# Delta-rule attention with two expert layers on one core: a shorter VectorE narrowing of the second part's weights, and later transposes

## The chip, the cores and the metric

The kernel runs on one core of a Trainium2 chip. The time is the device time of one execution in microseconds (us), and the number compared is the median of a few runs. The profile shows a single execution, so its span differs a little from the median. TensorE does the matrix products, VectorE (DVE) and ScalarE (ACT) the element-wise work on tiles in SBUF and PSUM, GpSimd (POOL) element-wise work in SBUF and some DMA issues, SyncE (SP) issues the other DMAs.

## The reference

The reference has three stages, cut here to what is computed. Inputs are `q`, `k`, `v` of 4 x 8 x 768 x 48, the weights `w_in` (384 x 2048), `w_out` (2048 x 384), `w_gate` (384 x 8), and `w1`, `w2` of eight experts. The dense weights come out of the reference's set-up as 64-bit floats; the other inputs are 32-bit.

```
for t in range(768):                       # 32 pairs of batch and head
    y[t]  = q[t] @ state
    state = state + beta[t] * outer(k_n[t], v[t] - k_n[t] @ state)
x = y as 3072 tokens x 384
h = x @ w_in
g = h * clip(h + 3, 0, 6) / 6
x = g @ w_out
logits = x @ w_gate                        # one expert per token: argmax
out[token] = gate * (relu(x @ w1[e]) @ w2[e])
```

## The kernel before, in words

Products that must be exact to 32 bits are made from a high and a low half: each weight and each activation is split into `H` (rounded by a ScalarE copy to the type that TensorE takes in one pass) and `L` (the rest, by a subtraction on GpSimd or VectorE), and three products H·H, H·L and L·H are added in PSUM.

The dense layer has 16 blocks of 128 of its 2048 hidden columns. The first seven (`NF1`) are multiplied in the first part of the program, beside the recurrence, for all tokens; their sum goes to the memory tensor `ypart`. The second part (from line 1298) does the other nine (`NF2` = 9) for six blocks of 512 tokens each. These six are called block 0 to block 5 below, the nine are rounds f = 0 to 8. A round makes `ph`, nine gate products of 512 columns on TensorE (lines 1316 to 1321), then `t` on ScalarE and VectorE, `gH` on ScalarE and `gL` on VectorE (1323 to 1328), and, two rounds later (`SK` = 2), twelve output products into the four `py` banks (1329 to 1336). After the last round `gather` adds `ypart` (1229) and `route` sorts the 512 tokens into the experts' slots. Then come the eight experts.

The weights arrive as 64-bit floats. `narrow` (lines 172 to 185) turns one tile of 128 x 384 of them into 32-bit floats: a DMA on SP's queue brings both halves into a `stage` tile (a ring of four), ScalarE writes the absolute value of the high words into an `nw` tile (a ring of three), and four VectorE operations follow: a maximum that bounds the exponent from below, a shift left by three with a mask, an operation that puts the top bits of the high word back, and one that adds the top three bits of the low word. `weights` (187 to 208) does one block: it narrows the `w_in` tile and splits it into `wiH` and `wiL` (ScalarE, GpSimd); narrows the `w_out` tile and splits it into `woH` and `woL`; transposes it on TensorE (`pwt`, three transposes) and copies the result to `wt` on ScalarE; and multiplies it with the router's weights (`pwc`, six products), copies eight columns (`wc`, VectorE) and splits those into the last columns of `woH` and `woL`. So each block is four steps, ended by the word "part". In the multiplication of the first seven blocks `narrow_first` does the same narrowing in another way: a scaled absolute value on ScalarE, a multiplication of the high words by zero on GpSimd, and two VectorE operations.

Of the nine blocks of the second part the first three (`NP` = 3) are prepared at the tail of the first part by `ahead_stream`, with `tags[0]` = "st". The other six (f = 3 to 8) are prepared in block 0's loop by `prepare` (tags[0] = "rst"): in round f, ahead of the gate products, block f+3 takes its first step, block f+2 its second, block f+1 its third and block f its fourth. Both use the same rings.

Each engine works through its instructions in a fixed order, which is made when the program is built. In the first part the order of the named streams is written out by hand (`ORDER`). Elsewhere a planner goes by the order of the text, and lets an instruction go ahead of an earlier one that it expects not to be ready; so instructions of `prepare` can stand between those at the tail of the first part. The expert weights (`load_expert`) are loaded into the same ring of stage tiles after the last narrowing.

Of the kernel before, what the change touches and what calls it, by code (L numbers as in the profile page):

```python
# [7 lines left out]
FP32 = mybir.dt.float32  # L8
# [4 lines left out]
ACTF = mybir.ActivationFunctionType  # L13
ALU = mybir.AluOpType
# [57 lines left out]
def kernel(ctx: ExitStack, tc: tile.TileContext, q, k, v, beta, w_in, w_out, w_gate, w1, w2, out):  # L72
# [21 lines left out]
    PE, ACT, DVE, POOL, DMA = [Defer(n, e) for n, e in (("pe", pe), ("act", act), ("dve", dve), ("pool", pool), ("dma", nc.sync))]  # L94
# [75 lines left out]
    def narrow(src_ap, sp, tags):  # L170

        t_ = sp.tile([128, 384, 2], I32, tag=tags[0], name="stage", bufs=tags[1])
        src = src_ap.bitcast(I32)
        if len(src.shape) == 3:
            yield DMA.dma_start(out=t_.rearrange("p (c f) two -> p c (f two)", c=src.shape[1]), in_=src)
        else:
            yield DMA.dma_start(out=t_.rearrange("p f two -> p (f two)"), in_=src)
        b_ = sp.tile([128, tags[4]], I32, tag=tags[2], name="nw", bufs=tags[3])[:, 0:384]
        bf = b_.bitcast(FP32)
        yield ACT.activation(bf, t_.bitcast(FP32)[:, :, 1], ACTF.Abs)  # L180
        yield DVE.tensor_scalar(bf, bf, 2.0 ** -15, None, ALU.max)
        yield DVE.tensor_scalar(b_, b_, 3, 0x3FFFFFFF, ALU.logical_shift_left, ALU.bitwise_and)
        yield DVE.scalar_tensor_tensor(b_, t_[:, :, 1], -(1 << 30), b_, ALU.bitwise_and, ALU.bitwise_or)
        yield DVE.scalar_tensor_tensor(b_, t_[:, :, 0], 29, b_, ALU.logical_shift_right, ALU.bitwise_or)
        return bf

    def weights(f, di, do, sp, tags, take, give):

        fs = slice(f * 128, (f + 1) * 128)
        t_ = yield from narrow(w_in.bitcast(I32).rearrange("(c p) f -> p c f", p=128)[:, :, f * 256:(f + 1) * 256], sp, tags)  # L190
        yield from split_ops(di, t_.rearrange("p (c f) -> p c f", c=KD))
        yield "part"
        t_ = yield from narrow(w_out[fs, :], sp, tags)
        yield from split_ops([x[:, 0:DM] for x in do], t_)
        yield "part"
        p_ = yield from take("pwt", t_)
        yield [PE.transpose(p_[:, c * 128:(c + 1) * 128], t_[:, c * 128:(c + 1) * 128], ident) for c in range(KD)]
        wt = sp.tile([128, tags[7]], FP32, tag=tags[5], name="wt", bufs=tags[6])[:, 0:DM]
        yield ACT.activation(wt, p_[:, 0:DM], ACTF.Copy)
        give(p_)  # L200
        yield "part"
        p2 = yield from take("pwc", wt)
        yield [PE.matmul(p2[:, 0:E], wt[:, c * 128:(c + 1) * 128], wg[:, c], start=c == 0, stop=c == KD - 1) for c in range(KD)]
        wc = sp.tile([128, E], FP32, tag="wc", name="wc")
        yield DVE.tensor_copy(wc, p2[:, 0:E])
        give(p2)
        yield from split_ops([x[:, DM:YW] for x in do], wc)
# [3 lines left out]
    NP = 3  # L211
# [809 lines left out]
    def bank(name):  # L1021
        return ps.tile([128, 512], FP32, tag="ps", name=name)
# [55 lines left out]
    def load_xt(rw, xt):  # L1078
        n = sum(height(rw))
        for c in range(KD):  # L1080
            p_ = bank("pxe")[:, 0:n]
            for t, r_ in enumerate(rw):
                m = r_.shape[0]
                pe.transpose(p_[:, t * 128:t * 128 + m], r_[:, c * 128:(c + 1) * 128], ident[0:m, 0:m])
            act.activation(xt[0][:, c, 0:n], p_, ACTF.Copy)
            dve.tensor_tensor(xt[1][:, c, 0:n], p_, xt[0][:, c, 0:n].bitcast(FP32), ALU.subtract)
        return xt
# [50 lines left out]
    def step(gen, n):  # L1138
        for _ in range(n):
            r = next(gen, None)  # L1140
            if r is not None:
                ready[id(gen)] = r
        return ready.get(id(gen))

    pre = load_expert(0, "a")
    with mx:
# [36 lines left out]
        def wi(x, f):  # L1183
            return (ahead["wi"][x][:, :, f * 128:(f + 1) * 128] if f < NP else wi1[x][:, :, (f - NP) * 128:(f - NP + 1) * 128])

        def wo(x, f):
            return ahead["wo"][x][:, f] if f < NP else wo1[x][:, f - NP]
# [4 lines left out]
        def load_x(b):  # L1192
            xt = x_tiles(b)
            for x in range(2):
                pool.dma_start(out=xt[x], in_=xd[x].rearrange("(c p) t -> p c t", p=128)[:, :, b * 512:(b + 1) * 512])
            return xt
# [9 lines left out]
        def prepare(f, parts=1):  # L1206

            if f not in range(NP, NF2):
                return
            if f not in prep:  # L1210
                prep[f] = weights(NF1 + f, [wi(x, f) for x in range(2)], [wo(x, f) for x in range(2)], wr,
                                  ("rst", 4, "rnw", 3, 384, "rwt", 2, DM), bank_now, lambda p_: None)
            for op in prep[f]:
                if op == "part":
                    parts -= 1
                    if not parts:
                        return
                    continue
                for o in (op if isinstance(op, list) else [op]):
                    o.now()  # L1220
# [66 lines left out]
        def pad_first():  # L1287

            pk = bank("pad")
            pe.matmul(pk[:, 0:E], oneb, cnt, start=True, stop=True)  # L1290
            pad = rp.tile([1, E], FP32, tag="pad", name="pad", bufs=1)
            dve.tensor_scalar(pad, pk[0:1, 0:E], -1.0, float(FIRST), ALU.mult, ALU.add)
            padb = const.tile([128, E], BF16, name="padb")
            dve.memset(padb, 0.0)
            dve.tensor_scalar(padb[0:1, 0:1], pad[:, 0:1], 0.0, None, ALU.max)
            counts.append(padb)

        row, first = None, {}
        for b in range(NT // 512):
            xt = nxt  # L1300
            if b + 1 < NT // 512:
                nxt = load_x(b + 1)
            if b == 1:
                step(pre, 1)
            py = [bank(f"py{t}") for t in range(4)]
            pend = []
            for f in range(NF2 + SK):
                if f == SK + 1 and row is not None:
                    step(route(b - 1, row), 2)
                if b > 1 and f % 2:  # L1310
                    step(pre, 1)
                if b == 0:
                    for n in range(4):
                        prepare(f + NP - n)
                if f < NF2:
                    ph = bank("ph")
                    n = 0
                    for c in range(KD):
                        for a, x in ((0, 0), (0, 1), (1, 0)):
                            pe.matmul(ph, wi(a, f)[:, c], xt[x][:, c], start=n == 0, stop=n == 3 * KD - 1)  # L1320
                            n += 1
                    t_ = gp.tile([128, 512], FP32, tag="t", name="t")
                    act.activation(t_, ph, ACTF.Relu, bias=half, scale=1.0 / 6.0)  # L1323
                    dve.scalar_tensor_tensor(t_, t_, 1.0, ph, ALU.min, ALU.mult)  # L1324
                    gH = gp.tile([128, 512], FP32R, tag="gH", name="gH", bufs=SK + 1)
                    gL = gp.tile([128, 512], FP32R, tag="gL", name="gL", bufs=SK + 1)
                    act.activation(gH, t_, ACTF.Copy)  # L1327
                    dve.tensor_tensor(gL, t_, gH.bitcast(FP32), ALU.subtract)  # L1328
                if f >= SK:
                    fp, gh, gl = pend.pop(0)  # L1330
                    for t in range(4):
                        ts_ = slice(t * 128, (t + 1) * 128)
                        o = py[t][:, 0:YW]
                        pe.matmul(o, gh[:, ts_], wo(0, fp), start=fp == 0, stop=False)  # L1334
                        pe.matmul(o, gh[:, ts_], wo(1, fp), start=False, stop=False)  # L1335
                        pe.matmul(o, gl[:, ts_], wo(0, fp), start=False, stop=fp == NF2 - 1)  # L1336
                if f < NF2:
                    pend.append((f, gH, gL))
                if b == NT // 512 - 1:
                    if f == SK + 1:  # L1340
                        pad_first()
                    if f == SK + 4:
                        first["rows"] = load_rows(0, slots, 0, FIRST, rp, "row2")
                    if f == NF2 - 1:
                        first["xt"] = load_xt(first["rows"], x_tiles(b + 1))
            row = gather(b, py)
# [144 lines left out]
```

## Time and profile before

| what | us |
|---|---|
| median of three runs (960.23 to 964.41) | 963.11 |
| time of the profiled execution | 965.32 |
| span of the profiled execution, first to last instruction | 963.6 |
| TensorE busy | 871.2 |
| VectorE busy | 575.1 |
| ScalarE busy | 549.3 |
| GpSimd busy | 440.8 |

Busy times are sums over instructions; products overlap, and a busy TensorE is not one at its peak. The chain that ended last is followed back from the last instruction, at each step to what released it. The granted clock is a share of 2.4 GHz: 1.00 is 2.4, 0.50 is 1.2. Nearly all operations of the helpers carry line 36, so they are told apart by tile names.

### The profile page before, as it was taken

What the parts mean: (1) busy time and instruction counts of PE and PEld (TensorE: products, weight loads), DVE (VectorE), ACT (ScalarE), POOL (GpSimd) and SP (SyncE); (2) the same over time, 40 slices, a digit from 0 to 9 for tenths busy, and PEclk for the clock granted to TensorE, in tenths of its full rate; (3) what the DMA queues carried; (4) which work ended last, traced back from release to release, by engine and by line L of the source; (5) the groups of instructions that cost most, each with busy time, mean ns of one, the idle gap of its engine ahead of it and who ended that gap; (6) DMA issues with size and microseconds to landing.
All of it is one profiled execution on the core that took longest, in us unless ns stands there. A gap on an engine that the chain in (4) does not pass through costs nothing.

```text
span 963.6 us, 27622 instructions
## 1 busy us (share of the span) xinstructions
PE 871.2 (90%) x11570; PEld 812.9 (84%) x11570; DVE 575.1 (60%) x1493; ACT 549.3 (57%) x1105; POOL 440.8 (46%) x423
## 2 busy tenths in 40 slices
PE   2425889999989999989899999999999999999996
PEld 2324889989989999988778988989899999999996
DVE  7898999979879797654785365554452221122221
ACT  5858888788978867655565333332325454255521
POOL 6676656455635424323441140321116744775751
PEclk9999999999999999999999999999999999999999
DMA  8789999999888767873653342241318633544400
GB/s 151 150 161 153 162 186 153 169 185 158 168 151 175 173 153 167 180 237 101 198 184 108 106 149 66 101 127 40 118 60 273 219 92 117 176 125 126 161 21 21
DMA packets 250918, 137.83 MB, mean 143 GB/s; under 512 B 195427, under 2 KB 235685, under 8 KB 250784
## 3 DMA queue, kind: packets, MB, share of 16 engines
q1 hardware_dynamic: 242960, 117.77, 53.7%
q0 software_dynamic: 7280, 17.41, 5.6%
q8 instruction: 92, 1.51, 0.7%
q10 hardware_dynamic: 544, 0.80, 0.2%
q14 instruction: 42, 0.34, 0.1%
HBM read 71.56 MB, written 35.50 MB: 111 GB/s over the span
## 4 chain that ended last, share of the span: by engine, by line
PE 73%; DVE 9%; issue 6%; ACT 5%; POOL 4%; DMA 1%; SPq 1%; POOLq 0%; ACTq 0%
PE ph L1320 11%; PE ph L1111 9%; PE ph L36 8%; PE py L36 8%; PE py L1335 4%; PE py L1334 4%; PE py L1336 4%; PE pz L1099 3%; PE pz L1101 3%; PE pz L1100 3%; PE pO L36 3%; PE pW L36 3%; DVE nw L36 2%; PE pP L36 2%; DVE nws L36 1%
## 5 line engine op out<-in xcount | busy, mean ns | idle before, releaser
L1115 DVE SCALAR_TENSOR_TENSOR hL<-ph,hH 128x384 fp32r<-128x384 f32 (+6 forms) x64 | 36.1, 564 | 163.5 <-ACT hH L1114 161.4
L36 POOL TENSOR_TENSOR gL<-t,gH 128x512 fp32r<-128x512 f32 (+1 forms) x48 | 56.3, 1174 | 108.8 <-ACT gH L36 80.7
L1114 ACT ACTIVATE hH<-ph 128x384 fp32r<-128x384 f32 (+6 forms) x64 | 31.6, 494 | 105.2 <-PE ph L1111 105.2
L1280 POOL DMA_INDIRECT slots<-row,di x24 | 23.9, 996 | 125.1 <-DVE di L1272 119.6
L1323 ACT ACTIVATE t<-ph,half 128x512 f32<-128x512 f32 x54 | 37.1, 688 | 75.8 <-PE ph L1320 71.2
L36 PE MATMUL ph<-xTH,wiH 128*128 128x256 f32 x252 | 75.3, 299 | 1.1 <-DVE t L36 1.0
L1324 DVE SCALAR_TENSOR_TENSOR t<-t,ph 128x512 f32<-128x512 f32 x54 | 37.1, 686 | 64.3 <-ACT t L1323 55.5
L1132 POOL DMA_INDIRECT out_dram<-yo,rw x29 | 28.1, 968 | 100.7 <-ACT yo L1131 96.4
L1099 PE MATMUL pz<-a2H,hH 128*128 128x384 f32 (+1 forms) x216 | 73.2, 339 | 0.4 <-ACT hH L1114 0.4
L1100 PE MATMUL pz<-a2L,hH 128*128 128x384 f32 (+1 forms) x216 | 72.4, 335 | 0.0
L1101 PE MATMUL pz<-a2H,hL 128*128 128x384 f32 (+1 forms) x216 | 72.4, 335 | 0.0
L36 PE MATMUL ph<-xTL,wiH 128*128 128x256 f32 x252 | 71.9, 285 | 0.2 <-DVE xTL L36 0.2
L36 PE MATMUL ph<-xTH,wiL 128*128 128x256 f32 x252 | 71.7, 285 | 0.0
L1328 DVE TENSOR_TENSOR gL<-t,gH 128x512 fp32r<-128x512 f32 x54 | 46.6, 864 | 32.7 <-ACT gH L1327 32.5
L36 DVE TENSOR_TENSOR Xp<-Xp,sub 128x31 f32<-128x31 f32 (+15 forms) x186 | 64.0, 344 | 2.7
L36 DVE TENSOR_TENSOR sub<-Bt,Xp 128x31 f32<-128x31 f32 (+15 forms) x186 | 62.0, 333 | 3.2
L152 POOL TENSOR_TENSOR a2L<-r,a2H 128x384 fp32r<-128x384 f32 x64 | 62.5, 1008 | 0.0
L36 PE MATMUL py<-woH,gH 128*128 128x392 f32 x168 | 61.0, 363 | 0.0
L152 POOL TENSOR_TENSOR a1L<-r,a1H 128x512 fp32r<-128x512 f32 x48 | 60.4, 1301 | 0.1
L36 PE MATMUL py<-woL,gH 128*128 128x392 f32 x168 | 57.6, 343 | 1.8 <-issue 1.8
L1111 PE MATMUL ph<-yTL,a1H 128*128 128x384 f32 (+5 forms) x168 | 58.3, 347 | 0.0
L1111 PE MATMUL ph<-yTH,a1L 128*128 128x384 f32 (+5 forms) x168 | 58.3, 347 | 0.0
(323 smaller groups left out, 3066.3 us busy)
## 6 DMA issues: line engine op xcount, KB each, us to landing
r<-in_moe_w_dram SPq DMA_DIRECT2D x32, 768.0 KB, 4.5
slots<-zrow SPq DMA_DIRECT2D x8, 784.0 KB, 5.5
stage<-in_moe_w_out_dram SPq DMA_DIRECT2D x16, 384.0 KB, 4.7
stage<-in_moe_w_in_dram SPq DMA_DIRECT2D x16, 384.0 KB, 3.6
row<-ypart SPq DMA_DIRECT2D x6, 784.0 KB, 4.4
ysave<-row SPq DMA_DIRECT2D x6, 784.0 KB
rw<-slots SPq DMA_DIRECT2D x24, 196.0 KB, 3.0
kr<-in_k_dram SPq DMA_DIRECT2D x24, 192.0 KB, 4.6
```

Of the source, the lines that this page charges most:

```text
L36: return self.fn(*self.a, **self.k)
L152: in_order(pool.tensor_tensor(dst[1], src_ap, dst[0].bitcast(FP32), ALU.subtract))
L1099: pe.matmul(o, hh[:, ts_], a2[0][:, fp], start=fp == 0, stop=False)
L1100: pe.matmul(o, hh[:, ts_], a2[1][:, fp], start=False, stop=False)
L1101: pe.matmul(o, hl[:, ts_], a2[0][:, fp], start=False, stop=fp == KF2 - 1)
L1111: pe.matmul(ph, a1[a][:, c, fs], xt[x][:, c, 0:n], start=k == 0, stop=k == 3 * KD - 1)
L1320: pe.matmul(ph, wi(a, f)[:, c], xt[x][:, c], start=n == 0, stop=n == 3 * KD - 1)
L1323: act.activation(t_, ph, ACTF.Relu, bias=half, scale=1.0 / 6.0)
L1328: dve.tensor_tensor(gL, t_, gH.bitcast(FP32), ALU.subtract)
L1334: pe.matmul(o, gh[:, ts_], wo(0, fp), start=fp == 0, stop=False)
L1335: pe.matmul(o, gh[:, ts_], wo(1, fp), start=False, stop=False)
L1336: pe.matmul(o, gl[:, ts_], wo(0, fp), start=False, stop=fp == NF2 - 1)
```

## The change

For the six blocks prepared in block 0's loop the narrowing is done as in the first part: the absolute value is scaled by 2 to the -112 on ScalarE, GpSimd multiplies the high words by zero in place, which leaves their top bit, and VectorE shifts the scaled value and joins that bit in one operation, then joins the low word's bits as before. Two VectorE operations per tile go, one GpSimd operation comes. In block 0's rounds the third and fourth step (transposes and router products) are issued behind the gate products and their `t`, `gH`, `gL` instead of ahead of them.

```diff
@@ narrow
-        yield ACT.activation(bf, t_.bitcast(FP32)[:, :, 1], ACTF.Abs)
-        yield DVE.tensor_scalar(bf, bf, 2.0 ** -15, None, ALU.max)
-        yield DVE.tensor_scalar(b_, b_, 3, 0x3FFFFFFF, ALU.logical_shift_left, ALU.bitwise_and)
-        yield DVE.scalar_tensor_tensor(b_, t_[:, :, 1], -(1 << 30), b_, ALU.bitwise_and, ALU.bitwise_or)
+        hi = t_.bitcast(FP32)[:, :, 1]
+        if tags[0] == "rst":
+            yield ACT.activation(bf, hi, ACTF.Abs, scale=2.0 ** -112)
+            yield POOL.tensor_scalar(hi, hi, 0.0, None, ALU.mult)
+            yield DVE.scalar_tensor_tensor(b_, b_, 3, t_[:, :, 1], ALU.logical_shift_left, ALU.bitwise_or)
+        else:
+            yield ACT.activation(bf, hi, ACTF.Abs)
+            yield DVE.tensor_scalar(bf, bf, 2.0 ** -15, None, ALU.max)
+            yield DVE.tensor_scalar(b_, b_, 3, 0x3FFFFFFF, ALU.logical_shift_left, ALU.bitwise_and)
+            yield DVE.scalar_tensor_tensor(b_, t_[:, :, 1], -(1 << 30), b_, ALU.bitwise_and, ALU.bitwise_or)
         yield DVE.scalar_tensor_tensor(b_, t_[:, :, 0], 29, b_, ALU.logical_shift_right, ALU.bitwise_or)
@@ the loop over the rounds
                 if b == 0:
-                    for n in range(4):
+                    for n in range(2):
                         prepare(f + NP - n)
                 if f < NF2:
                     ph = bank("ph")
...
                     dve.tensor_tensor(gL, t_, gH.bitcast(FP32), ALU.subtract)
+                if b == 0:
+                    for n in range(2, 4):
+                        prepare(f + NP - n)
                 if f >= SK:
```

## Rows read from the trace of the kernel before

**Rows 1.** The page: busy time by engine, and the chain's shares by engine.
```profile
PE 871.2 (90%) x11570; PEld 812.9 (84%) x11570; DVE 575.1 (60%) x1493; ACT 549.3 (57%) x1105; POOL 440.8 (46%) x423
PE 73%; DVE 9%; issue 6%; ACT 5%; POOL 4%; DMA 1%; SPq 1%; POOLq 0%; ACTq 0%
```
**Rows 2.** The chain in order of time (start us, us, what): starts of blocks 0, 1, 2.
```profile
469.65 4.47 PE ph L1320 x18
...
518.49 6.30 PE ph L1320 x27
...
557.11 6.30 PE ph L1320 x27
```
**Rows 3.** The chain, 486 to 507: the transposes' release, and two groups of gate products.
```profile
486.68 1.25 DVE nw L36
...
487.98 0.55 PE pwt L36 x3
488.53 0.57 PE pwc L36 x6
489.10 3.52 PE ph L1320 x9
...
504.96 2.19 PE ph L1320 x9
```
**Rows 4.** Waits (us in total, times, longest): 455 to 515, 469 to 519, 518 to 963.
```profile
PE pwt L36 <- DVE nw L36: 4.6, 4, 2.4
...
PE pwt L36 <- DVE nw L36: 2.2, 3, 1.9
...
PE pz L1099 <- ACT hH L1114: 0.4, 1, 0.4
```
**Rows 5.** Stretches: length, busy PE, PEld, DVE, ACT, POOL, then granted clock.
```profile
486.00:488.00 2.00, 0.10 (x2) 0.03 (x1) 1.97 (x5) 1.51 (x5) 1.56 (x2) 1.00 0.39 117
...
490.00:493.00 3.00, 3.00 (x9) 2.41 (x8) 2.92 (x8) 0.63 (x2) 0.00 (x0) 0.50 0.24 81
```
**Rows 6.** The chain at the tail of the first part, 460 to 470.
```profile
461.23 2.57 DVE nw L36 x3
...
463.93 0.52 PE pwt L36 x3
...
466.81 0.43 ACT gH L36
...
467.30 0.74 POOL gL L36
...
469.10 0.51 ACT yp L36
```
**Rows 7.** VectorE groups, 459 to 505 (busy us, mean ns), and the stretch 479.4 to 488.
```profile
L36 DVE TENSOR_SCALAR nw<-nw 128x384 int32<-128x384 int32 x13 | 7.8, 615 | 0.1
L36 DVE TENSOR_SCALAR nw<-nw 128x384 f32<-128x384 f32 x13 | 5.4, 426 | 0.4 <-ACT nw L36 0.4
...
479.40:488.00 8.60, 6.70 (x39) 5.92 (x38) 8.50 (x18) 4.21 (x11) 3.66 (x4) 1.00 0.40 126
```
**Rows 8.** By tile `stage`, whole span: ns min/median/max, first and last start.
```profile
L36 DVE SCALAR_TENSOR_TENSOR nw<-stage,nw x36: 544/554/1618, 413.8 to 503.2; 128x384 int32<-128x384 int32 x36
L36 ACT ACTIVATE nw<-stage x18: 534/544/557, 411.1 to 497.0; 128x384 f32<-128x384 f32 x18
...
L36 ACT ACTIVATE nws<-stage x14: 523/544/554, 10.8 to 111.9; 128x384 f32<-128x384 f32 x14
L36 POOL TENSOR_SCALAR stage<-stage x14: 1192/1220/2066, 11.4 to 115.5; 128x384 f32<-128x384 f32 x14
L36 DVE SCALAR_TENSOR_TENSOR nws<-nws,stage x14: 534/555/1345, 13.1 to 120.9; 128x384 int32<-128x384 int32 x14
```
**Rows 9.** GpSimd groups, 475.4 to 506: busy us, mean ns, idle before.
```profile
L36 POOL TENSOR_TENSOR woL<-nw,woH 128x384 fp32r<-128x384 f32 x5 | 5.2, 1047 | 3.6 <-ACT woH L36 3.6
L36 POOL TENSOR_TENSOR wiL<-nw,wiH 128x384 fp32r<-128x384 f32 x4 | 4.4, 1096 | 15.6 <-ACT wiH L36 15.6
L36 POOL TENSOR_TENSOR woL<-wc,woH 128x8 fp32r<-128x8 f32 x5 | 1.7, 336 | 0.1
```
**Rows 10.** Instructions in order of time, VectorE then GpSimd, 460 to 463.
```profile
460.14 0.35 DVE L36 TENSOR_SCALAR nw<-nw 128x384 f32<-128x384 f32 x1
...
461.70 1.62 DVE L36 SCALAR_TENSOR_TENSOR nw<-stage,nw 128x384 int32<-128x384 int32 x1
...
461.43 1.47 POOL L36 TENSOR_TENSOR gL<-t,gH 128x512 fp32r<-128x512 f32 x1 [2.02 <-ACT gH L36]
```
**Rows 11.** In order of time: ScalarE, GpSimd; then pieces of the chain.
```profile
478.57 1.43 ACT L36 ACTIVATE nw<-stage 128x384 f32<-128x384 f32 x3
...
482.53 1.00 POOL L36 TENSOR_TENSOR wiL<-nw,wiH 128x384 fp32r<-128x384 f32 x1 [7.20 <-ACT wiH L36]
504.42 1.00 POOL L36 TENSOR_TENSOR woL<-nw,woH 128x384 fp32r<-128x384 f32 x1 [2.24 <-ACT woH L36]
...
493.22 0.52 ACT wiH L36
...
507.14 0.18 PE py L1334
```

## The prediction

> **What bounds the kernel now.** I read the page's busy shares and its chain of waits first. TensorE is busy for 90% of the span and carries 73% of the chain that ended last [rows 1]. So a saving counts only where TensorE stands still, and the question is where it does so because of the narrowing that the change touches. The chain in order of time gives the three starts that matter: block 0 of the second part begins at 469.65, block 1 at 518.49, block 2 at 557.11 [rows 2]. Block 0 takes 48.84 us, block 1 38.62. Block 0 has six transpose groups (0.55 us) and six groups of router products (0.57) that block 1 has not [rows 3], 6 x 1.12 = 6.72. That leaves 48.84 - 38.62 - 6.72 = 3.50 us of lost time in block 0.
>
> The waits say where it goes. TensorE stands 2.2 us in three pieces, 1.9 the longest, before the transposes `pwt`, each time for the VectorE narrowing of `nw` [rows 4]. The long piece ends at 487.98, straight behind a narrowing instruction of VectorE. After it the granted clock is 0.50 in 490 to 493 (the 1.2 GHz level), after a stretch of 2 us in which TensorE was busy for 0.10 us [rows 5], and the nine gate products behind it cost 3.52 us where a later group takes 2.19: 1.33 more [rows 3]. 2.2 + 1.33 = 3.5, which is all of the excess.
>
> There is one more such wait, 2.36 us, the rest of the 4.6 that four waits make [rows 4]. It stands at the tail of the first part: the transposes of the last block prepared there start at 463.93, released by the third of a run of `nw` instructions that began at 461.23 [rows 6]. That narrowing itself is not changed, but VectorE does one of the second part's narrowings (block 3's) interleaved with it. Behind it TensorE works on without a gap to block 0 but for short waits for `gH`, `gL` and `yp` [rows 6], so what is won there moves block 0 forward.
>
> **The change, part by part.** (1) Six blocks are prepared in block 0's loop, two narrowings each, so twelve lose two VectorE operations. From 459 to 505 there are 26 of these, 13.2 us, of which 24 (12.2 us) belong to them [rows 7]. The two remaining VectorE operations keep their shape: 0.55 us each [rows 8]. VectorE is nearly full in just the stretch where TensorE stands: 8.50 of the 8.60 us from 479.4 to 488.0 [rows 7]. It does 18 instructions there; a narrowing has four, of which two go, so some eight of the 18 are dropped ones, and the narrowing that released TensorE at 487.98 should be through about 2 us earlier (8 x 0.35 less the 0.5 of the next paragraph). The scaled Abs costs what the plain one costs (0.544 us both) [rows 8].
>
> (2) Each narrowing gains one GpSimd operation that clears all but the top bit of the high words. The first part does the same operation in the same shape: 1.22 us median, 1.19 to 2.07 [rows 8]; twelve are 14.6 us (14.3 to 24.8). GpSimd has room: from 475.4 to 506 it is busy for 5.2 + 4.4 + 1.7 = 11.3 us and stands 15.6 us before `wiL` alone [rows 9]. Nine of the twelve fall there, 11.0 us, 22.3 of 30.6. On the latency of one narrowing I take 1.22 in and two operations out (0.35 each undisturbed, 0.51 in the mean: 0.70 to 1.02) [rows 7, 10]: 0.2 to 0.5 us longer each. It is covered by the distance between preparing and use: block f+3's gate weights are prepared in round f, three rounds of about 5.5 us ahead. The bounds of this edit run from 0 to the serial case under the rivals. What queues behind the new wait: on VectorE the next narrowing's operations, and `t` and `gL` of the round if they are placed behind a shift that waits for GpSimd; on GpSimd the subtractions `wiL` and `woL`, and two loads of the next x, which are needed only at 518.49. SP's queue feels it through the ring of four stage tiles: a load waits for the last VectorE operation of the narrowing four before. I count that at nothing for the same lead of three rounds; without it, it is the 0.2 to 0.5 above per load.
>
> (3) The last two of the four steps in a round move behind the gate. They issue three transposes and the copy `wt` on ScalarE; six router products, the copy `wc` on VectorE, and one small ScalarE and one small GpSimd operation; no DMA. TensorE then has nine gate products (2.19 us) to do before it can stand at a transpose, more than the longest wait of 1.9. On ScalarE and VectorE these steps now stand behind `t`, `gH` and `gL`; the router columns are wanted by the output products two rounds later, so this costs nothing unless a round's `gL` is later than that.
>
> The sum. In block 0 the 3.5 us can go wholly (with the wait the slow clock goes too) or not at all; I take 2.5, keeping 1.0 for a shorter wait at another place, because ordering by GpSimd's 1.22 us puts new hand-overs in. At the tail of the first part, two dropped operations stood ahead of the releasing one at a step of 0.27 us (two of four that start between 460.14 and 461.23 [rows 6, 10]), and a 1.62 us operation of the other narrowing stood between [rows 10]. The third of the run ends at 461.23 + 2.57 = 463.80 and takes 0.55, so it starts 1.55 behind 461.70. If all of that goes it is 0.54 + 1.55 = 2.1; if the new GpSimd operation falls beside the two that stay and holds one of them back by the 1.07 that the 1.62 has over 0.55, it is 1.0; at worst 0. I take 0.9. Together 3.4 us, with bounds 0 and 5.6. The profiled execution has a span of 963.6 and a time of 965.32, so it would come to 961.9; the median of the runs is 963.11, 2.2 lower, so the forecast for the median is 963.11 - 3.4 = 959.7. After block 0 TensorE waits in all 0.4 us visibly [rows 4], so what is won stays won.
>
> One row speaks against this sum: a narrowing operation with two inputs from SBUF took 1.62 us while GpSimd's `gL` ran for 1.47 beside it, against 0.55 alone [rows 8, 10]. The Trainium skill, "Advanced Engine Details and Errata", section Miscellaneous Facts (GPSIMD Details), says that GpSimd shares a read and a write interface with VectorE and conflicts with VectorE instructions in a 2-port mode or with two SBUF inputs. This row agrees with it; the rival that follows has its price from the row.
>
> **The rivals.** *A, VectorE is held back as much as it is relieved.* Twelve GpSimd operations, each holding one VectorE operation back by 1.07, are 12.8 us against 12.2 removed. Then VectorE is as late as today, the tail gains nothing, and only the new order helps: a wait of 1.9 partly covered, partly moved to a later place, 0.6 us of gain: 962.5. For it: the 1.62. Against it: in the first part the same shift has a median of 0.55 beside a GpSimd that is busier [rows 8].
> *B, everything goes.* 3.5 + 2.1 = 5.6: 957.5. For it: either half of the change alone covers 1.9 us. Against: it needs both places clean.
> *C, slower: the narrowings run one behind another through GpSimd.* GpSimd works in order; where a subtraction that waits for ScalarE stands ahead of the next narrowing's multiplication, one narrowing takes 0.54 + 1.22 + 1.10 + 0.52 + 1.05 and four hand-overs of 0.04 = 4.6 us [rows 8, 9, 11]. Nine of them from 478.57 on end at 520.0; the last block's transposes and router products (1.1) and twelve output products of 0.18 [rows 11] bring block 0's end to 523.3 instead of 518.5, and a slow clock after such waits costs 1.3 more: 968 to 969, I say 968.5. It decides from a step of 4.1 us per narrowing, where today's end is met ((518.5 - 2.2 - 1.1 - 478.6) / 9); today the step is (505.4 - 478.6) / 9 = 3.0. For it: GpSimd stood 7.2 us for `wiH` today [rows 11]. Against: three `nw` tiles let three narrowings overlap, and then GpSimd's own 2.3 us sets the step.
> *D, the move does nothing.* The planner orders each engine by what it expects to be ready, not by the text alone, and may leave the transposes where they were. Then the lighter VectorE alone shortens the waits: 1.6 us, 961.5.
>
> **How the numbers follow.** Forecast 0.46 (its own range 958 to 961.5), A 0.20, B 0.16, C 0.12, D 0.06. Without most of C the range is 956.0 to 966.5. About 0.5% (4.8 us) is what a measurement of this kernel tells from no change: faster than 958.3 is nearly all of B and the lower edge of the forecast, 0.20; slower than 967.9 most of C, 0.10; the rest 0.70.
>
> **What would show it.** Right: block 0 from its first gate product to block 1's first is near 46.3 us instead of 48.84; no wait of `pwt` for `nw` over 0.5 us; no stretch at 0.50 clock from 470 to 519; start of block 0 some 0.9 earlier. A shows as VectorE shifts of well over 0.55 on average, C as GpSimd at over 90% with `ph` or `py` waiting for `wiL` or `woL`. The prediction is wrong if block 0 is no shorter, or if the time changes outside block 0 and the tail ahead of it.

## The result: slower by half a per cent

The changed kernel takes 968.36 us (median of 13 runs, 966.49 to 971.29), the kernel before, in the same 13 rounds, 963.11. The ratio is 1.0053 with an interval of 1.0036 to 1.0070: 3.5 to 6.7 us slower, where 3.4 us faster was forecast and 966.5 was the upper end of the range. The profiled execution took 966.49 us, with a span of 964.4.

The page of the changed kernel answers to [rows 1]: VectorE 4 us less, GpSimd 17 us more, and of the chain two points less on TensorE, with "issue", ScalarE, GpSimd and DMA each one more.

```profile
PE 872.4 (90%) x11570; PEld 814.7 (84%) x11570; DVE 571.1 (59%) x1469; ACT 549.5 (57%) x1105; POOL 458.0 (47%) x435
PE 71%; DVE 9%; issue 7%; ACT 6%; POOL 5%; DMA 2%; SPq 0%; POOLq 0%; ACTq 0%; DVEq 0%
```

The span cannot be compared directly: what comes before the tail differs by some microseconds from one execution to the next (here the changed kernel is 3.6 us ahead at the last 512-column round of the first part). Two lengths inside one execution can. The **tail** runs from the start of ScalarE's `t` of that last round to block 0's first gate product; **block 0** from there to block 1's first gate product. Instructions in order of time (start us, us, engine, line, operation), the kernel before first, then the changed one:

```profile
458.81 0.69 ACT L36 ACTIVATE t<-ph,half 128x512 f32<-128x512 f32 x1 [1.24 <-PE ph L36]
...
469.65 0.50 PE L1320 MATMUL ph<-xH,wi0H 128*128 128x512 f32 x1 [0.59 <-ACT yp L36]
...
518.33 0.39 PE L1320 MATMUL ph<-xH,wi0H 128*128 128x512 f32 x1
```
```profile
455.22 0.69 ACT L36 ACTIVATE t<-ph,half 128x512 f32<-128x512 f32 x1 [1.24 <-PE ph L36]
...
469.61 0.50 PE L1326 MATMUL ph<-xH,wi0H 128*128 128x512 f32 x1 [0.59 <-ACT yp L36]
...
519.22 0.39 PE L1326 MATMUL ph<-xH,wi0H 128*128 128x512 f32 x1
```

The tail went from 10.84 to 14.39 us, block 0 from 48.68 to 49.61: +3.55 and +0.93, together +4.48. Block 1 takes 38.6 in both, and from its start to the end of the span there are 445.3 and 445.2 us. So all that can be seen of the loss lies in the two places that the forecast named, most of it in the tail.

**The tail.** TensorE stands 3.62 us before the transposes, against 2.36. In the chain of the changed kernel the narrowing ahead of them is the first part's own, and GpSimd's multiplication is in it:

```profile
456.88 1.23 POOL stage L36
458.11 0.02 issue
458.13 0.04 DVE nw L36
458.16 0.75 issue
458.91 0.61 DVE nw L36 x2
459.53 1.39 issue
460.92 0.56 DVE nw L36
461.47 0.14 issue
461.61 0.87 PE pwt L36 x3
```

Instruction by instruction (VectorE, then GpSimd) the reader sees why. The first operation of block 3's new narrowing stands in VectorE's order between the four of the unchanged one. It waits 0.51 us for GpSimd, and its 0.86 comes on top. Block 3's second one, started at 459.38, is then stretched to 1.61 beside `gL`, which GpSimd began late, behind two multiplications:

```profile
458.13 0.86 DVE L36 SCALAR_TENSOR_TENSOR nw<-nw,stage 128x384 int32<-128x384 int32 x1 [0.51 <-POOL stage L36]
459.38 1.61 DVE L36 SCALAR_TENSOR_TENSOR nw<-stage,nw 128x384 int32<-128x384 int32 x1
460.92 0.55 DVE L36 SCALAR_TENSOR_TENSOR nw<-stage,nw 128x384 int32<-128x384 int32 x1
...
456.88 2.39 POOL L36 TENSOR_SCALAR stage<-stage 128x384 f32<-128x384 f32 x2 [1.06 <-ACT nw L36]
459.23 1.35 POOL L36 TENSOR_TENSOR gL<-t,gH 128x512 fp32r<-128x512 f32 x1
```

The wait is 1.26 longer; the rest of the 3.55, 2.3 us, goes with the slow clock that followed it and did not follow the shorter wait in the profile before. Stretches (length, busy PE, PEld, DVE, ACT, POOL, then the granted clock), one of the kernel before, then three of the changed one: before, 1.00 of 2.4 GHz behind the wait; now 0.55 from 460 to 464, so mostly the 1.2 GHz level, and a second fall in block 0 after 488 to 490, where TensorE was busy for 0.43 of 2 us.

```profile
463.00:467.00 4.00, 3.07 (x21) 3.10 (x21) 3.93 (x9) 2.02 (x5) 1.01 (x1) 1.00 0.46 149
...
460.00:464.00 4.00, 2.39 (x10) 2.42 (x11) 2.77 (x5) 1.31 (x4) 1.87 (x2) 0.55 0.43 122
488.00:490.00 2.00, 0.43 (x5) 0.46 (x5) 1.68 (x4) 0.74 (x3) 2.00 (x3) 1.00 0.14 47
490.00:493.00 3.00, 3.00 (x16) 3.00 (x16) 2.97 (x4) 2.00 (x4) 3.00 (x3) 0.69 0.64 163
```

The 2.3 us are of this one execution. Two kernels below (narrowing alone, subtractions on VectorE) have the same wait, 3.62 and 3.63, and tails of 13.51 and 13.56: there the clock was back at 1.00 some three microseconds after the start of the transposes, here after more than five, and the wait cost 1.4 us more instead of 2.3.

**Block 0.** The waits of 440 to 520 (us in total, times, longest), and of all engines from 455 to 520: the transposes still wait for the narrowing, and VectorE now waits for GpSimd, as [rows 4] had no row for.

```profile
PE pwt L36 <- DVE nw L36: 7.0, 3, 3.6
...
DVE nw L36 <- POOL stage L36: 7.6, 9, 1.7
```

Two of the three, 0.98 and 2.39 us, lie in block 0, in place of 1.91 and twice 0.16. The groups of VectorE and GpSimd from 469 to 519 (busy us, mean ns, idle before), first of the kernel before, then of the changed one:

```profile
L36 DVE SCALAR_TENSOR_TENSOR nw<-stage,nw 128x384 int32<-128x384 int32 x19 | 11.5, 624 | 0.1
L36 DVE TENSOR_SCALAR nw<-nw 128x384 int32<-128x384 int32 x9 | 5.2, 588 | 0.0
L36 DVE TENSOR_SCALAR nw<-nw 128x384 f32<-128x384 f32 x9 | 4.1, 458 | 0.4 <-ACT nw L36 0.4
```
```profile
L36 DVE SCALAR_TENSOR_TENSOR nw<-nw,stage 128x384 int32<-128x384 int32 x9 | 9.1, 1015 | 5.4 <-POOL stage L36 5.4
L36 DVE SCALAR_TENSOR_TENSOR nw<-stage,nw 128x384 int32<-128x384 int32 x9 | 6.7, 750 | 0.1
L36 POOL TENSOR_SCALAR stage<-stage 128x384 f32<-128x384 f32 x9 | 12.4, 1388 | 1.1 <-ACT nw L36 1.1
```

Before, the narrowings held VectorE for 11.5 + 5.2 + 4.1 = 20.8 us. Now they hold it for 9.1 + 6.7 = 15.8 and let it stand 5.4 us for GpSimd: 21.2. The two dropped kinds of operation, 9.3 us, came back as a first operation of 1.015 us instead of 0.55, a second of 0.750, and the wait.

### The profile page after: what moved, and what is told of

Its sections match the earlier page's. It is cut to its first block, busy times and chain, and to the rows that moved or that the text cites. A ratio compares the mean times of both kernels' runs of the same rounds, so it can differ in the third digit from the quotient of the medians.

```text
span 964.4 us, 27615 instructions
## 1 busy us (share of the span) xinstructions
PE 872.4 (90%) x11570; PEld 814.7 (84%) x11570; DVE 571.1 (59%) x1469; ACT 549.5 (57%) x1105; POOL 458.0 (47%) x435
## 4 chain that ended last, share of the span: by engine, by line
PE 71%; DVE 9%; issue 7%; ACT 6%; POOL 5%; DMA 2%; SPq 0%; POOLq 0%; ACTq 0%; DVEq 0%
PE ph L1326 11%; PE ph L1117 9%; PE ph L36 8%; PE py L36 8%; PE py L1343 4%; PE py L1344 4%; PE py L1345 4%; PE pz L1105 3%; PE pz L1107 3%; PE pz L1106 3%; PE pO L36 3%; PE pW L36 2%; PE pP L36 1%; DVE nws L36 1%; PE pR L36 1%
## 5 line engine op out<-in xcount | busy, mean ns | idle before, releaser
L1334 DVE TENSOR_TENSOR gL<-t,gH 128x512 fp32r<-128x512 f32 x54 | 47.0, 870 | 33.2 <-ACT gH L1333 33.0
L36 PE MATMUL py<-woH,gL 128*128 128x392 f32 x168 | 58.5, 348 | 0.2 <-issue 0.2
```

The lines of the kernel that those rows point to most:

```text
L36: return self.fn(*self.a, **self.k)
```

## The experiments

Theory 1 was that the wait for GpSimd in VectorE's fixed order, and the longer chain of one narrowing, are what cost. The rivals: the moved steps (2), GpSimd's own work, through its queue and the interface that it shares with VectorE (3), and one cost that moves between the tail and block 0 (4). Each kernel has one profiled execution, with the two lengths in us as defined above; the last column adds what they differ from the kernel before (59.52).

| kernel | ratio to before, interval | wait at the tail | tail | block 0 | sum - 59.52 |
|---|---|---|---|---|---|
| before | 1 | 2.36 | 10.84 | 48.68 | 0 |
| changed | 1.0053, 1.0036 to 1.0070 | 3.62 | 14.39 | 49.61 | +4.5 |
| narrowing alone | 1.0101, 1.0070 to 1.0132 | 3.62 | 13.51 | 55.95 | +9.9 |
| move alone | 0.9986, 0.9964 to 1.0008 | 2.35 | 10.83 | 46.81 | -1.9 |
| three VectorE operations, no GpSimd | 0.9966, 0.9943 to 0.9990 | 2.56 | 12.34 | 45.07 | -2.1 |
| changed, tail in order | 1.0038, 1.0014 to 1.0063 | 1.17 | 11.47 | 53.75 | +5.7 |
| three, and an idle multiplication | 1.0023, 1.0002 to 1.0045 | 2.88 | 12.96 | 47.64 | +1.1 |
| changed, old narrowing at the tail | 0.9995, 0.9969 to 1.0021 | 2.36 | 12.38 | 50.27 | +3.1 |
| three, old at the tail | 0.9954, 0.9931 to 0.9976 | 2.35 | 10.84 | 45.58 | -3.1 |
| three, tail in order | 0.9945, 0.9922 to 0.9968 | 1.68 | 10.33 | 45.06 | -4.1 |
| bit on ScalarE | not readable | 0.99 | 10.67 | 45.15 | -3.7 |
| subtractions on VectorE | 0.9997, 0.9977 to 1.0017 | 3.63 | 13.56 | 44.95 | -1.0 |
| four `nw` tiles | 1.0023, 1.0003 to 1.0043 | 2.89 | 13.67 | 48.44 | +2.6 |
| old narrowing, moved, tail in order | 0.9975, 0.9956 to 0.9995 | 1.68 | 10.38 | 46.81 | -2.3 |

From block 1's start to the end of the span every kernel but one (bit on ScalarE) takes 445.2 to 446.2 us, so the sum tells most of the ratio. It is of one execution, though, and holds that execution's slow clock. The profiled one of "changed, old narrowing at the tail" was the slowest of its twelve, 969.01 against a median of 965.73.

Block 0 can be taken apart. In the eight kernels whose clock stays at 1.00 throughout it (all below "changed" but narrowing alone, changed with the tail in order or with the old tail, and four `nw` tiles) TensorE is busy for 44.45 to 44.90 us of it. What block 0 takes beyond that is TensorE's waits and, in the others, the slow clock behind them. The whole of block 0 as a stretch, changed, three VectorE operations, idle multiplication (columns as above):

```profile
469.61:519.22 49.61, 46.23 (x243) 41.66 (x244) 30.30 (x50) 31.85 (x66) 31.79 (x40) 0.97 0.65 198
...
469.50:514.60 45.10, 44.77 (x244) 40.24 (x245) 31.47 (x59) 31.67 (x66) 18.94 (x31) 1.00 0.69 210
...
471.50:519.10 47.60, 44.86 (x243) 40.22 (x244) 34.92 (x67) 31.88 (x66) 28.83 (x41) 1.00 0.66 199
```

Of the changed kernel's 4.54 us over three VectorE operations some 3.1 are thus waits of TensorE, and 1.5 slow clock.

**The two halves alone.** The narrowing without the move is the changed kernel without the second loop, and with the first one back to

```diff
-                    for n in range(2):
+                    for n in range(4):
```

> Only the narrowing is changed; all four steps of a round stay ahead of the gate products. Theory 1 (the narrowing with its GpSimd operation is the cause: at the tail a join that waits for GpSimd stands on VectorE between the operations of the unchanged narrowing, and in block 0 GpSimd is full): the transposes at the tail wait about 3.6 us with a slow clock behind them, block 0 starts as late as in the changed kernel, and the time is 1.003 to 1.007 of the kernel before. Theory 2 (the moved steps are the cause: the transposes hold the three nw tiles longer): the time is that of the kernel before, 0.998 to 1.001, and block 0 is no longer than its 48.8 us.

The move alone is the kernel before with both loops of the change.

> Only the steps are moved behind the gate products; the narrowing keeps its four VectorE operations. Theory 1: the wait at the tail stays near 2.4 us, block 0 takes 47 to 48.8 us instead of 48.84, and the time is 0.997 to 1.000 of the kernel before. Theory 2: block 0 takes 49.5 to 51 us and the time is 1.002 to 1.005.

Theory 2 is out: the move alone shortens block 0 by 1.87 us (its ratio is not clear of 1, at -0.14%). Little of that is wait. In block 0 the transposes still wait 1.8 us, where it was 2.2:

```profile
PE pwt L36 <- DVE nw L36: 1.8, 2, 1.0
```

But the long wait of 1.91 is now two, 0.98 and 0.86, and the clock stays at 1.00; about 1.5 of the 1.87 us are the slow clock that did not come. The narrowing alone loses 1.01%, beyond what theory 1 gave; in block 0 its transposes, ahead of the gate again, wait 1.8, 2.8 and 1.9 us, with a slow clock behind them. The change is a good half and a bad half, and the good half hid half of the bad one.

**No GpSimd at all.** VectorE does three operations: shift, join with the masked top bit, join with the low word.

```diff
-            yield POOL.tensor_scalar(hi, hi, 0.0, None, ALU.mult)
-            yield DVE.scalar_tensor_tensor(b_, b_, 3, t_[:, :, 1], ALU.logical_shift_left, ALU.bitwise_or)
+            yield DVE.tensor_scalar(b_, b_, 3, None, ALU.logical_shift_left)
+            yield DVE.scalar_tensor_tensor(b_, t_[:, :, 1], -(1 << 31), b_, ALU.bitwise_and, ALU.bitwise_or)
```

> The changed kernel with the GpSimd operation replaced: the scaled Abs, then a shift by three, a join with the masked top bit and the join with the low word, all three on VectorE; the steps are moved as in the change. Theory 1: no wait for GpSimd is left, the wait at the tail is 1.5 to 2.4 us, block 0 takes 46 to 48 us, and the time is 0.995 to 0.999 of the kernel before. Theory 2: block 0 takes 49 us or more and the time is 1.001 to 1.005.

Block 0 falls to 45.07, and no transpose waits for `nw` in it: one operation more on VectorE than in the change, 4.54 us less in block 0. That is also 3.61 less than before, and less than the 46 to 48 that were expected. Its tail is 1.5 longer than before, with nearly the same wait, 2.56; there the clock fell.

**The multiplication as a bystander.** The same kernel, with the multiplication into a tile that nobody reads.

```diff
             yield ACT.activation(bf, hi, ACTF.Abs, scale=2.0 ** -112)
+            junk = sp.tile([128, 384], FP32, tag="rjk", name="junk", bufs=1)
+            yield POOL.tensor_scalar(junk, hi, 0.0, None, ALU.mult)
             yield DVE.tensor_scalar(b_, b_, 3, None, ALU.logical_shift_left)
```

> As the kernel with three VectorE operations, which needs nothing of GpSimd, and GpSimd does the change's multiplication as well, into a tile that nobody reads: the work, its place and its use of the shared interface are there, the wait of VectorE for it is not. Theory 1 (the wait in VectorE's fixed order and the longer chain are what costs): block 0 stays at 45 to 46.3 us, 0 to 1.2 over the 45.07 without the multiplication, and the time is within 0.2% of that kernel's. Theory 3 (the shared interface stretches both engines, and GpSimd's queue is full): block 0 takes 48 us or more, the joins with the high word 0.9 us or more on average, and the time is 1.000 to 1.004 of the kernel before.

VectorE's groups from 469 to 519, first without the idle multiplication, then with it:

```profile
L36 DVE SCALAR_TENSOR_TENSOR nw<-stage,nw 128x384 int32<-128x384 int32 x18 | 13.7, 794 | 0.1
L1334 DVE TENSOR_TENSOR gL<-t,gH 128x512 fp32r<-128x512 f32 x9 | 6.9, 772 | 2.4 <-ACT gH L1333 2.2
```
```profile
L36 DVE SCALAR_TENSOR_TENSOR nw<-stage,nw 128x384 int32<-128x384 int32 x18 | 14.7, 853 | 0.1
L1336 DVE TENSOR_TENSOR gL<-t,gH 128x512 fp32r<-128x512 f32 x9 | 8.4, 939 | 2.2 <-ACT gH L1335 2.2
```

Block 0 is 2.57 longer and the time 0.57% more, though nobody waits for the result. That refutes theory 1 as the whole cause (0 to 1.2 was its bound) and falls just short of theory 3's 48 us and 0.9 us; the ratio lies in theory 3's range. So GpSimd's mere work costs block 0 2.57 us. It is not simply a part of the change's 4.54, for it comes by other waits of TensorE, for `gL` and `wc` instead of `nw`, and without a slow clock:

```profile
PE py L1347 <- DVE gL L1336: 1.6, 1, 1.6
PE pwt L36 <- DVE wc L36: 1.1, 1, 1.1
```

**Who is waited for.** The multiplication on ScalarE, a copy with scale 0.0. Behind the routing this kernel does other work than the rest (its time is 2142 us; that the copy loses the top bit is a guess that was not looked at), so only the two stages ahead of the routing can be read.

```diff
-            yield POOL.tensor_scalar(hi, hi, 0.0, None, ALU.mult)
+            yield ACT.activation(hi, hi, ACTF.Copy, scale=0.0)
```

> The changed kernel with the multiplication by zero on ScalarE instead of GpSimd: VectorE does two operations and waits for another engine as in the change, but GpSimd is left as before. Theory 1 (the wait in VectorE's fixed order is the cause, whoever is waited for): block 0 takes 48 us or more and the tail 12 or more, 1.001 to 1.005 of the kernel before. Theory 3 (GpSimd's work, by its queue and by the interface, makes most of it): block 0 takes 45 to 46.5 us, the joins with the high word 0.8 us or less on average, and the time is 0.993 to 0.998.

VectorE does the change's two operations and waits for another engine as there, but not long: the groups from 469 to 519.

```profile
L36 DVE SCALAR_TENSOR_TENSOR nw<-nw,stage 128x384 int32<-128x384 int32 x9 | 5.4, 622 | 1.7 <-issue 1.0 <-ACT stage L36 0.7
L36 ACT ACTIVATE stage<-stage 128x384 f32<-128x384 f32 x9 | 4.7, 549 | 0.0
```

Block 0 takes 45.15 and the tail 10.67. So a hand-over to another engine is not in itself what costs.

**GpSimd's queue or the interface.** In block 0's preparing VectorE does the subtractions for `wiL` and `woL`; GpSimd keeps the multiplications.

```diff
+    def split_dve(dst, src_ap):
+        yield ACT.activation(dst[0], src_ap, ACTF.Copy)
+        yield DVE.tensor_tensor(dst[1], src_ap, dst[0].bitcast(FP32), ALU.subtract)
...
-        yield from split_ops([x[:, 0:DM] for x in do], t_)
+        yield from (split_ops if tags[0] == "st" else split_dve)([x[:, 0:DM] for x in do], t_)
```

> The changed kernel with the subtractions for wiL and woL of the six blocks on VectorE instead of GpSimd: GpSimd keeps the multiplications (12 us in block 0) and loses 13 us, VectorE gains twelve operations of 0.55 us. If GpSimd's queue is the cause (the multiplication waits behind subtractions), block 0 falls to 45.5 to 47 us and the time to 0.996 to 0.999. If the shared interface is the cause, the multiplications and VectorE's operations still stretch each other, VectorE has more of them, and block 0 stays at 48.5 us or more, 1.001 or more.

```profile
L36 DVE SCALAR_TENSOR_TENSOR nw<-nw,stage 128x384 int32<-128x384 int32 x10 | 6.7, 676 | 2.6 <-POOL stage L36 2.6
L36 DVE SCALAR_TENSOR_TENSOR nw<-stage,nw 128x384 int32<-128x384 int32 x10 | 5.9, 609 | 0.0
L36 DVE TENSOR_TENSOR wiL<-nw,wiH 128x384 fp32r<-128x384 f32 x6 | 3.3, 551 | 0.4 <-ACT wiH L36 0.4
L36 POOL TENSOR_SCALAR stage<-stage 128x384 f32<-128x384 f32 x10 | 13.4, 1348 | 11.5 <-ACT nw L36 10.0 <-DMA stage<-in_moe_w_in_dram 1.2
```

Block 0 falls by 4.66 to 44.95, the shortest of all, with the multiplications in place and VectorE busier (33.2 us against 29.8 from 470 to 519). So it was neither VectorE's load nor the multiplication by itself, but the multiplications and the subtractions together on GpSimd. By which of two ways they cost, this run does not part: the wait for the multiplication falls from 5.4 to 2.6 us, as with an emptier queue, and the joins fall from 1.015 and 0.750 to 0.676 and 0.609, as with less of GpSimd's work beside them. The ratio, 0.9997, missed its 0.996 to 0.999; the tail stayed as it was, 13.56 us with a wait of 3.63.

**The ring.** `nw` tiles four instead of three, in both places where the ring is named.

> The changed kernel with four nw tiles instead of three. If the longer chain of one narrowing (Abs waits for a tile that a subtraction on GpSimd still reads) sets the step, block 0 falls to 48 us or less and the time to 0.999 to 1.002 of the kernel before. If GpSimd's own work and the stretching set it, more tiles change nothing: block 0 49 to 50.5 us, 1.003 to 1.007.

Between the two answers: block 0 48.44 instead of 49.61, ratio 1.0023; the transposes in block 0 wait 2.17 us instead of 3.37. In this execution the ring accounts for about a quarter of block 0's 4.54.

**The tail.** All operations of blocks 3 and 4 on VectorE get an order edge to the last one of the tail's own narrowing.

```diff
                 for o in (op if isinstance(op, list) else [op]):
-                    o.now()
+                    r = o.now()
+                    if f < NP + 2 and o.eng == "dve":
+                        tc.add_manual_dep(r.ins, behind[25].name, ...)
```

> The changed kernel, and on VectorE the narrowings of blocks 3 and 4 may start only behind the last operation of the last narrowing of the first part's tail. The GpSimd operations are all still there. Theory 1: the transposes at the tail wait under 1.5 us, no slow clock follows, block 0 starts 2.5 to 4 us earlier against the tail's last full round than in the changed kernel, block 0 itself still takes 49 to 50.5 us, and the time is 0.998 to 1.001 of the kernel before. Theory 3 (it is not the order but the interface that VectorE and GpSimd share: VectorE's operations are stretched beside GpSimd wherever they stand): the wait at the tail stays at 2.4 us or more and the time at 1.003 or more.

The wait falls from 3.62 to 1.17 with every GpSimd operation still there; so at the tail it is the order. But TensorE then waits 1.4 us for `gL` of GpSimd, and block 0 takes 53.75. That is not for longer waits: in block 0 the transposes wait as long as in the changed kernel (3.4 us, the longest 2.4), and VectorE as long for GpSimd (5.4). It is the clock, which falls at the end of the tail, behind the wait for `gL`, and stays low for block 0's first five microseconds; behind the transposes it falls again, for longer than in the changed kernel. The wait, and a stretch of each (columns as above):

```profile
PE pwt L36 <- DVE nw L36: 3.4, 2, 2.4
...
471.00:475.00 4.00, 4.00 (x11) 3.03 (x10) 0.17 (x1) 0.67 (x2) 3.17 (x7) 0.50 0.96 288
494.00:498.00 4.00, 4.00 (x14) 4.00 (x15) 3.27 (x6) 2.82 (x8) 4.00 (x4) 0.50 0.59 196
```

Theory 1 had said that no slow clock follows, and 49 to 50.5 us; the ratio 1.0038 missed its 0.998 to 1.001 as well. The opposite cut keeps the old narrowing for blocks 3 and 4:

```diff
-        if tags[0] == "rst":
+        if tags[0] == "rst" and tags[8]:        # tags[8]: f > 4
```

> The changed kernel with the old narrowing kept for blocks 3 and 4, whose three narrowings stand at the first part's tail. Theory 1 (two separate costs, 3.5 us at the tail and 0.9 in block 0): the tail from its last full round takes 10.8 us again, block 0 49 to 50.5, and the time is 0.999 to 1.002 of the kernel before. Theory 4 (one cost that moves between the two places, as in the run with the tail in order): block 0 takes 52 us or more and the time is 1.003 or more.

The wait is 2.36 again and the ratio 0.9995, as theory 1 said; block 0 stays long, 50.27, with 2.35 us of waits and a clock of 0.50 for some seven microseconds behind them. In this execution the tail took 12.38 with the same wait that gave 10.84 before: the clock fell behind it, where it stayed at 1.00 in the profile before. The stretch in question (columns as above):

```profile
464.95:466.95 2.00, 2.00 (x8) 2.00 (x7) 1.97 (x5) 1.31 (x3) 0.24 (x1) 0.50 0.93 326
```

**What beats both.** Three operations with the old narrowing at the tail, with the two edits above; then three operations with the tail in order; and the order alone, with the old narrowing and the move.

> Three VectorE operations without GpSimd for blocks 5 to 8, the old four for blocks 3 and 4, and the steps moved. Theories 1 and 3: the tail takes 10.8 us as before, block 0 45 to 46 us, together 3 us less than before: 0.995 to 0.998 of the kernel before. Theory 4: the tail's gain comes back in block 0, and the sum is that of the kernel with three operations throughout, 57.4 us.

> Three VectorE operations without GpSimd for all six blocks, the steps moved, and on VectorE the narrowings of blocks 3 and 4 only behind the tail's last own narrowing. Theories 1 and 3: the tail takes 8.5 to 10 us, block 0 45 to 47 us, 3 to 5 us less than before: 0.993 to 0.997. Theory 4: block 0 takes 49 us or more and the time is that of the kernel before.

> The old narrowing with its four VectorE operations throughout, the steps moved, and on VectorE the narrowings of blocks 3 and 4 only behind the tail's last own narrowing. If the interleaving at the tail costs a wait of 1.3 us or more even with the old narrowing, the wait for the transposes falls from 2.36 to about 1.2 us and the tail to 9.7 us; block 0, with as much VectorE work as before in a shorter lead, takes 47 to 49 us; 0.996 to 1.000. If what is won at the tail comes back in block 0, the sum of the two is 57.6 us as with the moved steps alone.

Three operations with the tail in order are at 0.9945 and with the old tail at 0.9954, both clear of the kernel before; between them the intervals do not decide. The first of these tails, 10.33, is over the 8.5 to 10 that were expected. The two without the three operations show what each part is worth: the order edge 0.45 us of tail at no cost in block 0 (46.81 with and without it), where 1.1 was expected. So nothing here needs theory 4: in the two runs in which block 0 grew against the changed kernel as the tail shrank (53.75 and 50.27), its waits did not grow; the slow clock lasted longer.

## Why the prediction was wrong

- **What bounds.** Right: TensorE's waits at the tail and in block 0 carry it, and 445 us behind block 0 did not move. The 3.5 us that could go in block 0 are there as well: three VectorE operations without GpSimd take 3.61 off it.
- **The step that failed: GpSimd's operation was priced at "0.2 to 0.5 us longer each", "covered by the distance between preparing and use".** Block 0, forecast 2.5 us shorter, got 0.93 longer. I looked at GpSimd's room in sum (22.3 of 30.6 us) and not at its order, nor at what more of its work does to the operations beside it. In block 0 a multiplication waits behind subtractions, and the subtraction behind it waits for VectorE, which waits for the multiplication. The narrowing that released TensorE at 489.57 began with its Abs at 483.88; GpSimd began its multiplication at 485.11, behind `woL`, and needed 1.54 us; the first join took 1.34 beside `wiL`, the second 0.87: 5.6 us from the Abs to the end, where the narrowing that released TensorE took 4.4 before (483.56 to 487.93), so 1.2 longer and not 0.2 to 0.5. Of the 5.6 about 0.7 is the place behind `woL`, and 1.4 is what the three operations took beyond 1.22, 0.55 and 0.55. The lead of three rounds was no cover; one reason is the ring of three tiles, which lets Abs start only when an earlier subtraction is done, but four tiles took only a quarter of the loss away.
- **Two operations of "0.55 us each".** They took 1.015 and 0.750 in block 0. The medians of [rows 8] did not carry over to a stage in which GpSimd has this much more to do; why the first part's stayed short was not looked at.
- **The tail, -0.9 us, "at worst 0".** It was +3.55, and 1.26 of that is wait; I gave no reason for the bound. I let two of block 3's operations drop out of VectorE's order and one "stand between"; in their place came one that waits. That a wait in a fixed order holds the operations behind it was in the text, but for `t` and `gL`, not for the unchanged narrowing.
- **The slow clock.** I had it vanish with the waits. It came twice in the profiled execution: about 2.3 us at the tail (1.4 in two kernels with the same wait), 1.5 in block 0 (eleven output products in 3.49 us against 1.96 at 0.178 each).
- **The move.** Right in its sign; that 1.87 us came where a wait of 1.9 was to be covered is luck. The waits fell by only 0.4 us, and the rest is the slow clock that did not follow two shorter ones.
- **The rivals.** A had the stretching (joins of 1.015 and 0.750) but no loss. C had the queue and the sign, and its mark shows where it matters, from 478 to 490, where GpSimd is busy for 11.04 of 12 us; but what waits there is `pwt` for `nw`, not `ph` or `py` for `wiL` or `woL`. Its 968.5 is near the 968.36 by chance: its step of 4.1 us per narrowing was not reached (506.2 - 477.5, by nine: 3.2), and it put no loss at the tail, where most of it was.

The Trainium skill, "Advanced Engine Details and Errata", section Miscellaneous Facts (GPSIMD Details), has GpSimd conflict with VectorE instructions in a 2-port mode or with two SBUF inputs. The idle multiplication agrees: joins from 0.794 to 0.853 us, `gL` from 0.772 to 0.939. The shift, which has one input, got longer as well, from 0.452 to 0.519; whether it runs in the 2-port mode no run here shows. With the bit on ScalarE the first join is at 0.622, but the second at 0.791 is no shorter than with three VectorE operations.

That the same 2.36 us wait was followed by a slow clock in one execution and not in three others (before, move alone, three with the old tail) stays unexplained. So does about 0.8 us of the 5.25 between the medians, within the ratio's interval. How much of block 0's loss is the place in GpSimd's queue, and how much the longer operations beside it, stays open too.

## What to carry to other kernels

Work taken off a full engine and given to an engine with room in sum may cost more than it saves, if the other engine works in order and already stands in the same chain: ask what its new instruction queues behind, what runs beside it, and who on the first engine stands behind the join. Before dropping two operations for a hand-over, try dropping one and handing nothing over. And judge an edit by the stage's length inside one execution, half by half, before trusting that a combined change has one sign; and read the waits in it beside the length, since the slow clock behind the same wait came in one execution and not in another.

## What the runs showed of the hardware that was not expected

- An operation on GpSimd that no instruction waits for lengthened block 0 by 2.57 us; VectorE's two-input operations beside it were 7 and 22% longer on average.
- A wait of TensorE costs twice when the clock falls after it: at the tail 3.62 us cost 2.3 more in one execution and 1.4 in two, 2.36 us cost 1.5 more in one execution and nothing in three. In block 0 one wait of 1.91 us was followed by the slow clock, two of 0.98 and 0.86 were not.
- The multiplication by zero in place takes 1.35 to 1.39 us on GpSimd in block 0, where it took 1.22 in the first part; a ScalarE copy of the same shape takes 0.549, but the kernel with it does other work behind the routing.
